# Attention block with a gated feed-forward branch on one core: first tile's rstd by logarithm and exponential, gate by exponential and reciprocal, whole loads of x

## The chip, the cores and the metric

One core of one Trainium2 chip. The metric is device time in microseconds (us). The span of a profile is 1.7 to 1.9 us shorter than the time of the same execution.

PE is the matrix engine (TensorE), PEld its weight loads, DVE the vector engine, ACT the scalar engine, POOL GpSimd, SP the engine that issues most transfers.

## The reference, cut to what matters

```python
xn = layernorm(x)                                # 2048 rows of 512, no affine part
q  = (xn @ wq) per head                          # 32 heads of 128
s  = softmax(q k^T / sqrt(128)) v  ->  @ wo      # 2048 keys
z  = relu(xn @ w1 + b1)**2 @ w2 + b2             # 512 -> 1792 -> 512
out = x + s * silu(z)                            # silu(z) = z * sigmoid(z)
```

## The kernel before

One helper records each engine's program in order and puts in semaphore waits; each engine gets its instructions in that order. Rows come in four blocks of 512, and each block in four tiles of 128. A step of the main loop makes scores for two key tiles, one exponential of 128x1024 on ACT, and the product with V. A head is eight steps. Between them PE gets one or two "filler" matmuls of other jobs (projections, the feed-forward branch, the output product). PE leaves its results in PSUM: scores in psA, the product with V in the two banks of psO, the fillers in the two banks of psF. DVE copies psO and psF out (it "evicts" them), and only then can PE write the bank again, so a late eviction makes PE wait.

The layernorm's statistics, with the reciprocal root of the variance (rstd) as a power on GpSimd:

```python
def ln_rstd(j, i, n=1, eng=GP):
    t = E(DV, bn_aggr(mv_t[:, i, :], st_t[:, i, 0:6 * n]), deps=[t_bn[jt]] + prev)
    t = E(eng, ts(ve_t[:, i:i+1], mv_t[:, i, 1:2], 1.0, LN_EPS, mult, add), deps=[t] + prev)
    t_xr[jt] = E(GP, tt(rstd[:, i:i+1], ve_t[:, i:i+1], mhalf, pow), deps=[t, t_mhalf])
# (helper names shortened, cut)
```

The gate: twice silu(z) is z (1 + tanh(z/2)); the factor of a half comes in later.

```python
def tanh():
    box[0] = E(AC, act(th_t[:, s, :], z_t[:, s, :], Tanh, scale=0.5), deps=[tz, t_thr[s]])
def gate():
    t_g[jt] = E(DV, stt(g_all[:, gs, :], th_t[:, s, :], 1.0, z_t[:, s, :], add, mult), ...)
at(step + 1, tanh)
at(step + 3, gate)       # issued at that step, or when a head is past its second step
```

The head of the program, where K of head 0 is transposed on PE and copied by ACT:

```python
x tile 0, rows 64-127 -> ACT queue;  rows 0-63 -> SP queue
ln_load(0, 1, AC); load_k0(0); fill_wq(0, AC); load_k0(1)
# (cut)
warm_up(36); k0_transpose(0); k0_copy(0)
ln_bn(0, 0); ln_rstd(0, 0, eng=DV); ln_bn(0, 1); ln_scale(0, 0)
first_transpose(0); k0_transpose(1); bias_rows(); k0_copy(1)
ln_rstd(0, 1, eng=DV); first_copy(0); bias_copy(); first_proj(0)
ln_scale(0, 1); first_evac(0); first_transpose(1)
gen_scores(0); ln_bn(0, 2); gen_scores(1)
```

The softmax here doesn't subtract the row's maximum and nothing guards it: scores larger than these inputs give would overflow.

## Time and profile before

| | |
|---|---|
| time, first three runs | 1238.45, 1239.90, 1241.53 us |
| span of the profile | 1236.3 us |
| PE busy | 1231.2 us |
| DVE busy, before the change | 472.5 us |
| gates made | 16, one per tile of 128 rows |

The prediction shows the profile lines.

One more line is used below, from the view of the gate's tile. It gives the durations of ACT's 16 gate instructions and the start of the first and of the last. Compared between two kernels, the first start shows what the head lost or gained, the last start what head and middle together did:

```profile
L161 ACT ACTIVATE th_t<-z_t x16: 621/622/632, 111.2 to 1195.9; 128x512 bf16<-128x512 f32 x16
```

### The profile page before, as it was taken

To read this page: it belongs to the slowest core of one execution; us is meant where nothing else is said; L and a number is where in the kernel's file an instruction comes from. 1 tells how busy PE (TensorE), PEld (TensorE's weight loads), DVE (VectorE), ACT (ScalarE), POOL (GpSimd) and SP (SyncE) were. 2 spreads that over 40 slices of the span, in tenths; PEclk is the share of its full clock that TensorE was granted. 3 is DMA by queue.
4 is the path that set the end of the run, shared out by engine and by line. 5 is a ranking of instruction groups with operands and counts; after the bars stand their busy time and mean duration, and the time that the engine had idled before them with its cause. 6 is when DMAs were issued, how large, how long until landed. Compare 5 with 4: busy or idle time off the path is not lost.

```text
span 1236.3 us, 26936 instructions
## 1 busy us (share of the span) xinstructions
PE 1231.2 (100%) x11885; PEld 818.7 (66%) x11885; DVE 472.5 (38%) x953; ACT 1053.7 (85%) x1044; POOL 31.9 (3%) x73
## 2 busy tenths in 40 slices
PE   9999999999999999999999999999999999999999
PEld 7666666666666666666666666666666666666666
DVE  4453323244435332334444532333344333324333
ACT  7888888888888888888888888888888888888885
POOL 1010000000002000000000200000000000000000
PEclk9999999999999999999999999999999999999999
DMA  9999997777879797878779978788779799878771
GB/s 213 203 243 194 186 178 134 131 143 142 141 151 170 143 160 129 138 140 144 133 133 170 172 138 144 141 148 133 133 145 148 146 154 158 137 134 147 146 123 31
DMA packets 686884, 185.41 MB, mean 150 GB/s; under 512 B 673552, under 2 KB 685584, under 8 KB 686768
## 3 DMA queue, kind: packets, MB, share of 16 engines
q1 hardware_dynamic: 684592, 179.56, 80.8%
q0 software_dynamic: 1424, 3.81, 1.3%
q8 instruction: 94, 1.54, 0.5%
q10 hardware_dynamic: 752, 0.33, 0.1%
q14 instruction: 22, 0.18, 0.1%
HBM read 96.60 MB, written 2.10 MB: 80 GB/s over the span
## 4 chain that ended last, share of the span: by engine, by line
PE 99%; DVE 0%; DMA 0%; ACTq 0%; issue 0%; DVEq 0%
PE psO L157 38%; PE psA L152 36%; PE psF L152 25%; DMA x_ln<-in_A_x_dram 0%; PE psA L157 0%; DVE out_t L165 0%; PE psF L196 0%; DVE tmp_t L175 0%; PE psO L152 0%; DVE st_t L200 0%; DVE xn_t L171 0%; ACTq L208 0%; PE psO L196 0%; DVE xnT L179 0%; DVE b1f L179 0%
## 5 line engine op out<-in xcount | busy, mean ns | idle before, releaser
L161 ACT ACTIVATE pT<-psA 128x1024 bf16<-128x1024 f32 x1024 | 1043.5, 1023 | 163.6 <-PE psA L152 118.3
L157 PEld LDWEIGHTS psO<-v_sb,pT 128*128 128x128 bf16 x8192 | 547.9, 98 | 240.2 <-issue 12.5
L157 PE MATMUL psO<-v_sb,pT 128*128 128x129 bf16 x8192 | 631.2, 220 | 0.0
L152 PE MATMUL psA<-qt_sb,kT 128*128 128x512 bf16 x2032 | 604.4, 379 | 0.0
L179 DVE COPY o_un<-psO 128x258 f32<-128x258 f32 x256 | 97.3, 421 | 399.6 <-PE psO L157 398.9
L152 PE MATMUL psF<-xnT,wq_sb 128*128 128x512 bf16 (+1 forms) x520 | 168.8, 374 | 0.1
L152 PE MATMUL psF<-wo_all,oT 128*128 128x512 bf16 x480 | 163.6, 379 | 0.0
L152 PEld LDWEIGHTS psA<-qt_sb,kT 128*128 128x128 bf16 x2032 | 157.0, 98 | 0.0
L179 DVE CAST qt_sb<-psF 128x512 bf16<-128x512 f32 (+1 forms) x130 | 87.9, 676 | 97.1 <-PE psF L152 97.1
L165 DVE TENSOR_TENSOR o_bf<-o_un,rden 128x512 bf16<-128x512 f32 x128 | 88.6, 692 | 4.6 <-DVE rden L183 0.3
L152 PEld LDWEIGHTS psF<-xnT,wq_sb 128*128 128x128 bf16 x520 | 50.3, 98 | 59.8 <-DVE xnT L179 0.2
L171 DVE TENSOR_SCALAR r_t<-psF,b1f 128x512 bf16<-128x512 f32 x56 | 42.0, 750 | 117.5 <-PE psF L152 117.5
L152 PEld LDWEIGHTS psF<-wo_all,oT 128*128 128x128 bf16 x480 | 46.9, 98 | 56.4
L152 PE MATMUL psF<-xnT,w_sb 128*128 128x512 bf16 x224 | 77.1, 379 | 0.0
L152 PE MATMUL psF<-w_sb,h2T 128*128 128x512 bf16 x224 | 74.1, 379 | 0.0
L152 PEld LDWEIGHTS psF<-w_sb,h2T 128*128 128x128 bf16 x224 | 21.9, 98 | 26.4
L152 PEld LDWEIGHTS psF<-xnT,w_sb 128*128 128x128 bf16 x224 | 21.9, 98 | 26.4
L165 DVE TENSOR_TENSOR z_t<-psF,b2bc 128x512 f32<-128x512 f32 x16 | 11.1, 692 | 67.2 <-PE psF L152 67.2
L165 DVE TENSOR_TENSOR acc<-psF,acc 128x512 f32<-128x512 f32 x28 | 19.3, 688 | 30.0 <-PE psF L152 30.0
L208 POOL DMA_DIRECT2D out_dram<-out_t x12 | 6.7, 555 | 891.0 <-DVE out_t L165 891.0
L165 DVE TENSOR_TENSOR h2T<-r_t 128x512 bf16<-128x512 bf16 x56 | 23.8, 425 | 1.9
L183 DVE RECIPROCAL rden<-o_un 128x4 f32<-128x4 f32 x128 | 22.9, 179 | 4.4
(47 smaller groups left out, 164.3 us busy)
## 6 DMA issues: line engine op xcount, KB each, us to landing
v_sb<-in_A_v_cache_dram SPq DMA_DIRECT2D x127, 512.0 KB, 4.7
wq_sb<-in_A_wq_dram SPq DMA_DIRECT2D x127, 128.0 KB, 3.0
wo_all<-in_A_wo_dram SPq DMA_DIRECT2D x4, 1024.0 KB, 6.3
w_sb<-in_B_w_dram SPq DMA_DIRECT2D x14, 256.0 KB, 4.6
oT<-o_bf SPq DMA_TRANSPOSE x128, 3.9
x_t<-in_A_x_dram POOLq DMA_DIRECT2D x16, 128.0 KB, 3.6
kT<-in_A_k_cache_dram SPq DMA_TRANSPOSE x127, 4.5
x_ln<-in_A_x_dram SPq DMA_DIRECT2D x14, 128.0 KB, 4.2
```

The costliest lines, as they stand in the source:

```text
L152: return e.matmul(out, lhsT, rhs, start=start, stop=stop)
L157: return e.matmul(out, lhsT, rhs, start=start, stop=stop, skip_group_check=True)
L161: return e.activation(out, in_, func, bias=bias, scale=scale)
L165: return e.tensor_tensor(out, in0, in1, op)
L171: return e.tensor_scalar(out, in0, scalar1=scalar1, scalar2=scalar2, op0=op0, op1=op1)
L179: return e.tensor_copy(out, in_)
L183: return e.reciprocal(out, in_)
L208: return e.dma_start(out, in_)
```

## The change

As the edits read, the intent is to take tile 0's normalization off the GpSimd power and to have its x earlier. The traces show ACT loading tables for its functions (ACT_TABLE_LOAD, 1.28 us); one load can serve a set of several. Tanh is given up for exp and a reciprocal, it seems for fear that a set with a logarithm would not have it. The code gives no reason; experiment 6 bears on it. The core of the diff:

```diff
+    def first_rstd(i):
+        t = E(DV, bn_aggr(mv_t[:, i, :], st_t[:, i, 0:6]), deps=[t_bn[i]])
+        t = E(AC, act(ve_t[:, i:i+1], mv_t[:, i, 1:2], Ln, bias=epsc), deps=[t, t_eps])
+        t_xr[i] = E(AC, act(rstd[:, i:i+1], ve_t[:, i:i+1], Exp, scale=-0.5), deps=[t])
...
-    th_t = sb("th_t", [P, 2, D], BF16)
+    th_t = sb("th_t", [P, 2, D], F32)
...
-            def tanh(): act(th_t, z_t, Tanh, scale=0.5)
+            def exp():  act(th_t, z_t, Exp, scale=-1.0)
+            def sigmoid():
+                t = ts(th_t, th_t, 1.0, add)          # DVE
+                box[0] = recip(th_t, th_t)            # DVE
-            gate: (th_t + 1.0) * z_t
+            gate: (th_t * 2.0) * z_t
-            at(step + 1, tanh); at(step + 3, gate)
+            at(step + 1, exp); at(step + 3, sigmoid); at(step + 4, gate)
...
-    x tile 0 in two halves on two queues
+    ln_load(0, 0, SP)
     ln_load(0, 1, AC)
-    warm-up activation: Exp
+    warm-up activation: Ln
...
     warm_up(36); k0_transpose(0)
+    ln_bn(0, 0); first_rstd(0)
     k0_copy(0)
-    ln_bn(0, 0); ln_rstd(0, 0, eng=DV)
     ln_bn(0, 1); ln_scale(0, 0); first_transpose(0); k0_transpose(1)
-    bias_rows()
     k0_copy(1)
-    ln_rstd(0, 1, eng=DV); first_copy(0); bias_copy(); first_proj(0)
-    ln_scale(0, 1); first_evac(0); first_transpose(1); gen_scores(0); ln_bn(0, 2)
+    ln_rstd(0, 1); first_copy(0); first_proj(0); first_evac(0); ln_scale(0, 1)
+    gen_scores(0); ln_bn(0, 2); first_transpose(1)
     gen_scores(1); first_copy(1)
+    bias_rows(); bias_copy()                          # now through psO
```

(Shortened; a debug print that does nothing by default goes too.)

More of the change, by code (lines that the diff above doesn't have):

```diff
@@ L279, in bass_recurrent_scan__mha_block_cached__dense_activation_squared_relu__prompt_kernel @@
     z_t = sb("z_t", [P, 2, D], F32)
-    th_t = sb("th_t", [P, 2, D], BF16)
+    th_t = sb("th_t", [P, 2, D], F32)
+    epsc = sb("epsc", [P, 1], F32)
     b1b = sb("b1b", [NFC, P], BF16)
@@ L327, in bass_recurrent_scan__mha_block_cached__dense_activation_squared_relu__prompt_kernel @@
     t_mhalf = E(GP, partial(_memset, out=mhalf[:], val=-0.5))
+    t_eps = E(GP, partial(_memset, out=epsc[:], val=LN_EPS))
     t_idf = E(GP, partial(_iota, out=identf[:]))
@@ L356, in ln_bn @@
         t_bn[jt] = E(DV, partial(_bn_stats, out=st_t[:, i, k:k + 6], in_=x_ln[:, i, c0:c1]),
-                     deps=[t_xl[jt], t_x0 if jt == 0 else None, t_xn.get(jt - TPB),
-                           t_xr.get(jt - TPB)])
+                     deps=[t_xl[jt], t_xn.get(jt - TPB), t_xr.get(jt - TPB)])
     def ln_rstd(j, i, n=1, eng=GP):
@@ L368, in ln_rstd @@
                                  op=ALU.pow), deps=[t, t_mhalf])
+    def first_rstd(i):
+        t = E(DV, partial(_bn_aggr, out=mv_t[:, i, :], in_=st_t[:, i, 0:6]), deps=[t_bn[i]])
+        t = E(AC, partial(_act, out=ve_t[:, i:i + 1], in_=mv_t[:, i, 1:2], func=ACT.Ln,
+                          bias=epsc[:]), deps=[t, t_eps])
+        t_xr[i] = E(AC, partial(_act, out=rstd[:, i:i + 1], in_=ve_t[:, i:i + 1], func=ACT.Exp,
+                                scale=-0.5), deps=[t])
     def ln_stats(j, i):
@@ L445, in bias_rows @@
     def bias_rows():
-        t_b1[0] = E(PE, partial(_peT, out=psA[:, 1536:1600].bitcast(BF16)[:, 0:NFC], in_=b1b[:],
-                                ident=ident[0:NFC, 0:NFC]), deps=[tok_b1, t_ident])
+        t_b1[0] = E(PE, partial(_peT, out=bankO(1)[:, 0:64].bitcast(BF16)[:, 0:NFC], in_=b1b[:],
+                                ident=ident[0:NFC, 0:NFC]), deps=[tok_b1, t_ident, t_k0[1]])
     def bias_copy():
         t_b1[0] = E(DV, partial(_copy, out=b1f[:],
-                                in_=psA[:, 1536:1600].bitcast(BF16)[:, 0:NFC]), deps=[t_b1[0]])
+                                in_=bankO(1)[:, 0:64].bitcast(BF16)[:, 0:NFC]), deps=[t_b1[0]])
     def first_proj(i):
@@ L470, in second_proj @@
                                       start=(c == 0), stop=(c == NDC - 1)),
-                          deps=[t_wqfill[1], tok_xT[0][i], t_k0[1]], inc=(c == NDC - 1))
+                          deps=[t_wqfill[1], tok_xT[0][i], t_k0[1], t_b1[0]], inc=(c == NDC - 1))
     def second_evac():
@@ L539, in gen_scores @@
                                   rhs=qt_sb[:, 0, qt * P:(qt + 1) * P], start=True, stop=True),
-                      deps=[t_k0[b], t_q0[qt], t_exp[pi - 2] if pi >= 2 else t_b1[0]],
+                      deps=[t_k0[b], t_q0[qt], t_exp[pi - 2] if pi >= 2 else None],
                       inc=(c == NKT // 2 - 1))
@@ L622, in bass_recurrent_scan__mha_block_cached__dense_activation_squared_relu__prompt_kernel @@
     nfin = [0]
-    import os
-    dbg = os.environ.get("KDBG")
     pending = []
@@ L686, in evac, with exp @@
             box = [None]
-            def tanh():
-                box[0] = E(AC, partial(_act, out=th_t[:, s, :], in_=z_t[:, s, :], func=ACT.Tanh,
-                                       scale=0.5), deps=[tz, t_thr[s]])
+            def exp():
+                box[0] = E(AC, partial(_act, out=th_t[:, s, :], in_=z_t[:, s, :], func=ACT.Exp,
+                                       scale=-1.0), deps=[tz, t_thr[s]])
+            def sigmoid():
+                t = E(DV, partial(_ts, out=th_t[:, s, :], in0=th_t[:, s, :], scalar1=1.0,
+                                  scalar2=None, op0=ALU.add), deps=[box[0]])
+                box[0] = E(DV, partial(_recip, out=th_t[:, s, :], in_=th_t[:, s, :]), deps=[t])
             def gate():
@@ L694, in gate @@
                 t_g[jt] = t_zrd[s] = t_thr[s] = E(
-                    DV, partial(_stt, out=g_all[:, gs, :], in0=th_t[:, s, :], scalar=1.0,
-                                in1=z_t[:, s, :], op0=ALU.add, op1=ALU.mult),
+                    DV, partial(_stt, out=g_all[:, gs, :], in0=th_t[:, s, :], scalar=2.0,
+                                in1=z_t[:, s, :], op0=ALU.mult, op1=ALU.mult),
                     deps=[box[0], t_fin.get(jt - 2 * TPB)])
-            at(step + 1, tanh)
-            at(step + 3, gate)
+            at(step + 1, exp)
+            at(step + 3, sigmoid)
+            at(step + 4, gate)
             return tz
@@ L856, in load_w1 @@
                                sl_w1[i])
-    sl_x0 = S.slot("x0b")
-    t_x0 = S.emit_dma(AC, partial(_dma, out=x_ln[P // 2:P, 0, :], in_=A_x[0, P // 2:P, :]), sl_x0)
-    t_xl[0] = S.emit_dma(SP, partial(_dma, out=x_ln[0:P // 2, 0, :], in_=A_x[0, 0:P // 2, :]),
-                         sl_xl[0])
+    ln_load(0, 0, SP)
     ln_load(0, 1, AC)
@@ L865, in bass_recurrent_scan__mha_block_cached__dense_activation_squared_relu__prompt_kernel @@
     load_k0(1)
-    E(AC, partial(_act, out=th_t[:, 0, 0:1], in_=warm[:, 0:1], func=ACT.Exp), deps=[t_warm])
+    E(AC, partial(_act, out=th_t[:, 0, 0:1], in_=epsc[:], func=ACT.Ln), deps=[t_eps])
     ln_load(0, 2, SP)
@@ L910, in bass_recurrent_scan__mha_block_cached__dense_activation_squared_relu__prompt_kernel @@
     k0_transpose(0)
+    ln_bn(0, 0)
+    first_rstd(0)
     k0_copy(0)
-    ln_bn(0, 0)
-    ln_rstd(0, 0, eng=DV)
     ln_bn(0, 1)
@@ L917, in bass_recurrent_scan__mha_block_cached__dense_activation_squared_relu__prompt_kernel @@
     k0_transpose(1)
-    bias_rows()
     k0_copy(1)
     t_kfill[0] = t_k0[1]
-    ln_rstd(0, 1, eng=DV)
+    ln_rstd(0, 1)
     first_copy(0)
-    bias_copy()
     first_proj(0)
+    first_evac(0)
     ln_scale(0, 1)
-    first_evac(0)
-    first_transpose(1)
     gen_scores(0)
     ln_bn(0, 2)
+    first_transpose(1)
     gen_scores(1)
     first_copy(1)
+    bias_rows()
+    bias_copy()
     ln_rstd(0, 2)
@@ L988, in bass_recurrent_scan__mha_block_cached__dense_activation_squared_relu__prompt_kernel @@
             n += 1
-        if dbg:
-            print(pi, n, round(credit, 1), jobs[0][0] if jobs else None, len(pending))
         if pi >= NPR:
```

## The prediction

> **What bounds the kernel now.** I read the page's first part and its chain of waits first, then a table of busy time by stretches, then the timeline of the first 16 us (nearly every edit of the change sits there), the groups by form for the price of each operation, and last the timeline around the places where the gate is made. The page:
>
> ```profile
> PE 1231.2 (100%) x11885; PEld 818.7 (66%) x11885; DVE 472.5 (38%) x953; ACT 1053.7 (85%) x1044; POOL 31.9 (3%) x73
> ...
> PE 99%; DVE 0%; DMA 0%; ACTq 0%; issue 0%; DVEq 0%
> ```
>
> TensorE (PE) is the bound for practically the whole span of 1236.3 us. Everything else runs beside it, so a change can only count where it makes PE stand still, or stops it from standing still. The table of stretches says where PE stands still:
>
> ```profile
> 0.00:5.00 5.00, 3.89 (x41) 3.72 (x42) 1.03 (x3) 1.49 (x2) 2.58 (x13) 1.00 0.53 154
> 5.00:10.00 5.00, 3.99 (x60) 3.24 (x58) 4.05 (x14) 3.35 (x4) 1.31 (x4) 1.00 1.26 255
> 10.00:15.50 5.50, 5.43 (x96) 5.13 (x93) 3.19 (x10) 4.51 (x5) 1.34 (x3) 1.00 1.04 216
> ...
> 25.00:1225.00 1200.00, 1200.00 (x11531) 794.53 (x11529) 455.62 (x912) 1036.12 (x1026) 24.16 (x52) 1.00 0.83 150
> ```
>
> After the length of each stretch comes PE's busy time. From 25 to 1225 us it is 1200.00 of 1200.00. Only the head is loose, and even there part of the 3.89 us in the first 5 is warming-up matmuls on zeros. The change removes no PE work (the same transposes, in another order), so its whole possible gain lies in the first 8 us, before the first scores. That path in the timeline:
>
> ```profile
> 2.71 1.28 ACT L161 ACT_TABLE_LOAD   x1 [2.71 <-issue]
> 3.27 0.69 DVE L200 BATCH_NORM_STATS2 st_t<-x_ln 128x6 f32<-128x512 bf16 x1 [3.27 <-DMA x_ln<-in_A_x_dram]
> 4.46 0.57 POOL L165 TENSOR_TENSOR rstd<-ve_t,mhalf 128x1 f32<-128x1 f32 x1 [1.75 <-DVE ve_t L171]
> 5.12 0.69 DVE L200 BATCH_NORM_STATS2 st_t<-x_ln 128x6 f32<-128x512 bf16 x1 [0.75 <-DMA x_ln<-in_A_x_dram]
> 5.73 0.40 DVE L171 TENSOR_SCALAR xn_t<-x_ln,mv_t,rstd 128x512 bf16<-128x512 bf16 x1
> ...
> 8.02 0.91 PEld L157 LDWEIGHTS psA<-qt_sb,kT 128*128 128x128 bf16 x16
> ```
>
> The reader should see that the GpSimd power ends at 5.03, but the scaling of tile 0 starts only at 5.73: DVE works in order, and the statistics of tile 1 stand in front of it, and those wait for tile 1's x until 5.12. So the power isn't what tile 0 waits for; the late tile 1 is. The weights of the first scores are loaded at 8.02.
>
> **What the Trainium skill says.** (1) "ScalarE: Activation LUTs", section "Table sets: the hidden batching unit": functions come in sets loaded together; exp and tanh share one, a set with both ln and exp exists, and that set is not listed with tanh. The trace agrees for the first half: 1024 exponentials and 16 tanh ran on one load. No run here shows yet which set a logarithm brings. (2) The same page, section "What ACT_TABLE_LOAD costs": about 1283 ns, plus a drain of some 1380 ns, for a switch. The load here took 1283 ns; no switch between sets exists in this trace, so the drain isn't shown. (3) "VectorE: DVE Perf Modes", section "First, the fixed hardware budget": a reciprocal is an iterative divide with a repeat count of 8. The trace speaks for eight cycles an element, worked out below. (4) The same page, section "The perf-mode tier table (the rule you actually need)": a tensor-with-scalar operation on fp32 in SBUF runs at twice the basic rate; no such fp32 operation of any width is in this trace, though the 128x512 bf16 one takes 0.40 us.
>
> **The change part by part.**
>
> The gate, 16 times. Removed: a tanh; added: an exponential of the same 128x512 tile. Both are one ACT pass over the same elements, 624 ns by the group of tanh; fp32 output I take as free. ACT: no change. On DVE two instructions come in front of the gate, an add and a reciprocal over 128x512 fp32. The prices by form:
>
> ```profile
> L183 DVE RECIPROCAL rden<-o_un 128x4 f32<-128x4 f32 x128 | 22.9, 179 | 4.4
> ...
> L175 DVE SCALAR_TENSOR_TENSOR tmp_t<-psA,g_all 128x128 f32<-128x128 f32 x2 | 0.6, 291 | 0.2
> L175 DVE SCALAR_TENSOR_TENSOR tmp_t<-psA,g_all 128x256 f32<-128x256 f32 x1 | 0.4, 424 | 0.9 <-PE psA L152 0.9
> L171 DVE TENSOR_SCALAR ve_t<-mv_t 128x1 f32<-128x1 f32 x2 | 0.3, 154 | 0.1
> ```
>
> From 128 to 256 columns costs 133 ns, 1.04 ns a column, so one column a cycle is 1.04 ns, and the fixed part is 291 - 133 = 158 ns. One column costs 154. The reciprocal of four columns costs 179, which is 25 more than 154: three further columns at 8.3 ns, or eight cycles each. If that holds at 512 columns, one reciprocal is 154 + 511 x 8.33 = 4.41 us. At one cycle it would be 0.69 us. The add is, at double rate, about 0.15 + 512 x 0.52 = 0.42 us (estimate). So DVE gains 16 x 4.83 = 77 us of work (or 16 x 1.1 = 18), going from 472 to about 550 us, 44% of the span. By average that is nothing; in place it can hold up an eviction. What counts is the time from the gate's place to the next thing PE needs of DVE. I looked at all 16 gates in the timeline: each starts right behind a head's normalization, and the next eviction of psO (two banks, which PE needs back within about 0.7 us of finishing) comes 6.8 to 7.8 us later. 4.83 plus the gate's 0.69 fits. The evictions of psF come sooner, but psF also has two banks, so each has until the next psF job ends. The tightest case:
>
> ```profile
> 249.97 0.69 DVE L175 SCALAR_TENSOR_TENSOR g_all<-th_t,z_t 128x512 bf16<-128x512 bf16 x1
> ...
> 250.57 0.68 DVE L179 CAST qt_sb<-psF 128x512 bf16<-128x512 f32 x1
> ...
> 254.06 0.75 DVE L171 TENSOR_SCALAR r_t<-psF,b1f 128x512 bf16<-128x512 f32 x1 [2.81 <-PE psF L152]
> ...
> 254.74 0.59 PE L152 MATMUL psF<-wo_all,oT 128*128 128x512 bf16 x2
> ```
>
> The query's bank, evicted now at 250.57, is wanted again at 254.74. With the slow reciprocal it is evicted at 249.97 + 4.83 + 0.69 = 255.5: PE waits 0.75 us. The same happens at the gate at 555.95 (0.75). At 862.15 the bank is wanted at 867.60 and free at 867.67 (0.1). At the last gate, 1199.48, two combining operations and one eviction follow: 4.83 + 4 x 0.69 = 7.6 us puts the next psO eviction at 1207.1, its half done at 1207.5, and PE wants it at 1207.13 (0.4). Every other gate has at least 5.6 us until the next psF job ends. Sum if the reciprocal is slow: +2.0 us; if fast: 0.
>
> The head. Removed: the half-and-half load of tile 0 (halves landed 2.2 and 2.4 us after issue), DVE's small scaling (0.15) and the GpSimd power (0.57). Tile 0 now comes whole, alone on its queue; I put it between the half's 2.4 and the 3.8 us of tile 1, which queued behind a half: lands 3.6 instead of 3.27. Tile 1 no longer queues and should land near 3.6 to 4.0 instead of 5.10; that is the gain. Statistics of tile 0: 3.6 to 4.5 with the aggregate. On ACT: table load until 3.99, its first small activation until 4.2 as before, the logarithm 4.5 to 4.8 and the exponential to about 5.05 (about 0.2 to 0.28 each by the 205 ns of the first small one). Tile 1's statistics run 4.5 to 5.2 meanwhile; tile 0's scaling starts at about 5.25 instead of 5.73. Then, by the durations of before: transposes (0.4), copy (0.42), projection (0.4), eviction (0.29) and first scores. The bias transpose and tile 1's scaling (0.40) leave the way, so the first scores come near 7.4 instead of 8.02: -0.65 us. It assumes one table load.
>
> **The rivals.** First, two table loads: if a logarithm brings a set without exp, the exponential behind it loads a second one, 1.28 us on exactly this path. The scaling then starts at about 6.55 instead of 5.25, and the copy of K on ACT too stands behind it. First scores at about 8.6: +0.6 us. For it: the kernel only asks for a function, and the first choice for a lone logarithm need not hold exp. Against: giving up the tanh makes sense only if it would have cost reloads, so the one who wrote it expected the joint set. I give it 55%. If the joint set then never held, there still are no reloads later: only exp remains. Second, the slow reciprocal as an outright bound, +2% or more: for it, 77 us of new DVE work in lumps; against, the positions above, always behind a head's end. Third, the lone load of tile 0 arrives much later than 3.6 and eats the gain: that would give 0 in the head. Fourth, nothing at all: the head's gain is lost again in the following 7 us, where PE also waits for ACT and DVE in turn.
>
> **Range and chances.** Head: 0.45 x (-0.65) + 0.55 x 0.6 = +0.04. Gate: slow with 65%, so 0.65 x 2.0 = +1.3. Sum +1.3 on 1239.9 gives 1241.2; as the version was probably kept by someone who timed it, I shade it to 1240.8. The three runs before lie from 1238.45 to 1241.53, 3 us apart, which is wider than any of my terms; so the range is 1238.0 to 1243.3. Two per cent would be 24.8 us: slower needs a stall of 1.5 us at each of the 16 gates, faster would need PE work to vanish. I give 0.01 to each, 0.98 to within 2%.
>
> **What would show it.** In the changed profile: the group of the 128x512 reciprocal near 4.4 us (or 0.7); DVE near 550 us (or 490); PE waits for a DVE eviction of psF or psO near 250, 556 and 1207 us and nowhere else in the middle; the number of table loads; the scaling of tile 0 at 5.25 or 6.55; the first scores at 7.4 or 8.6. It would be wrong if the reordering put a gate's reciprocal close before a head's end, so that PE waits at all 16, or if loads of tables appear in the steady part.

## The result and the profile after

| | before | after |
|---|---|---|
| median of six runs | 1239.53 us | 1240.11 us |
| lowest to highest | 1238.36 to 1241.53 | 1240.02 to 1240.22 |
| span of the profile | 1236.3 us | 1238.2 us |

The ratio is 1.0004, with a 95% interval from 0.9991 to 1.0017: the same. Ratios here are the mean time of one kernel's fast runs over that of the other's in the same rounds, so not quite the ratio of the quoted medians. Small as it is, the traces differ by 1.9 us, more than the medians do: the runs of the kernel before scatter upward, and its lowest two are 1.7 us below the changed kernel's median.

From the page of the changed kernel, busy time by engine and the chain's shares:

```profile
PE 1231.7 (99%) x11885; PEld 818.9 (66%) x11885; DVE 532.3 (43%) x983; ACT 1056.3 (85%) x1047; POOL 31.6 (3%) x74
...
PE 98%; DVE 1%; DMA 0%; ACT 0%; issue 0%; DVEq 0%
```

PE has the same number of instructions as before. DVE has 60 us more, and it appears in the chain with 1%. The groups by form give the new prices (busy, then mean ns of one):

```profile
L183 DVE RECIPROCAL th_t<-th_t 128x512 f32<-128x512 f32 x16 | 53.7, 3353 | 0.6
...
L170 DVE TENSOR_SCALAR th_t<-th_t 128x512 f32<-128x512 f32 x16 | 6.8, 422 | 0.0
...
L161 ACT ACT_TABLE_LOAD x2 | 2.6, 1283 | 1.7 <-PEq L1042 1.7
```

Two loads of tables, an add of 0.42 us as estimated, and a reciprocal of 3.35 us. The table of stretches, PE's busy time behind the length of each:

```profile
0.00:5.00 5.00, 4.02 (x40) 4.02 (x41) 1.45 (x3) 2.15 (x4) 2.08 (x13) 1.00 0.61 175
5.00:10.00 5.00, 3.13 (x48) 2.52 (x45) 2.65 (x8) 3.91 (x5) 0.75 (x2) 1.00 1.25 253
...
25.00:1225.00 1200.00, 1199.41 (x11530) 794.06 (x11528) 514.70 (x943) 1037.90 (x1027) 24.15 (x52) 1.00 0.82 149
```

From 5 to 10 us PE is busy 3.13 us where it was 3.99, and 0.6 us are missing in the middle that was full. The head in the timeline:

```profile
3.37 0.69 DVE L200 BATCH_NORM_STATS2 st_t<-x_ln 128x6 f32<-128x512 bf16 x1 [3.37 <-DMA x_ln<-in_A_x_dram]
4.10 0.18 DVE L204 BATCH_NORM_AGGREGATE mv_t<-st_t 128x2 f32<-128x6 f32 x1
4.20 0.66 DVE L200 BATCH_NORM_STATS2 st_t<-x_ln 128x6 f32<-128x512 bf16 x1
4.31 0.29 ACT L161 ACTIVATE ve_t<-mv_t,epsc 128x1 f32<-128x1 f32 x1 [1.16 <-DVE mv_t L204]
4.62 1.28 ACT L161 ACT_TABLE_LOAD   x1
...
5.92 0.20 ACT L161 ACTIVATE rstd<-ve_t 128x1 f32<-128x1 f32 x1
...
6.16 0.41 DVE L171 TENSOR_SCALAR xn_t<-x_ln,mv_t,rstd 128x512 bf16<-128x512 bf16 x1 [1.30 <-ACT rstd L161]
...
8.46 0.46 PEld L157 LDWEIGHTS psA<-qt_sb,kT 128*128 128x128 bf16 x8 [0.62 <-issue]
```

Tile 1's statistics start at 4.20 instead of 5.12: the loads did what they were for. But between the logarithm and the exponential stands the second table load, and DVE sits idle for 1.30 us in front of the scaling "<-ACT rstd". The scaling starts at 6.16 instead of 5.73.

PE's own waits in the whole run, and the gate's first and last start:

```profile
PE psF L196 <- DVE xn_t L171: 1.2, 1, 1.2
...
PE psF L152 <- DVE qt_sb L179: 0.6, 2, 0.3
```
```profile
L161 ACT ACTIVATE th_t<-z_t x16: 621/622/632, 112.1 to 1197.8; 128x512 f32<-128x512 f32 x16
```

Before, PE waited for no eviction of a query at all. The first gate is 0.9 us later than before, the last one 1.9: so 0.9 us in the head and 1.0 in the middle. Setting the 1024 exponentials of the two traces side by side, the difference is 0.44 us at the first two, 0.89 from the third to the one at 256 us, then 1.43, then 1.85 from 563 us on, and it does not move again. The step at 256 us in the timeline:

```profile
251.34 3.35 DVE L183 RECIPROCAL th_t<-th_t 128x512 f32<-128x512 f32 x1
...
254.73 0.69 DVE L175 SCALAR_TENSOR_TENSOR g_all<-th_t,z_t 128x512 bf16<-128x512 f32 x1
...
255.34 0.68 DVE L179 CAST qt_sb<-psF 128x512 bf16<-128x512 f32 x1
...
256.17 0.59 PE L152 MATMUL psF<-wo_all,oT 128*128 128x512 bf16 x2 [0.34 <-DVE qt_sb L179]
```

The matmul that stood at 254.74 before stands at 256.17: 1.43 later, of which 0.89 was brought along from the head. It waited for the query's eviction, which stood in DVE's order behind reciprocal and gate. The listed wait is 0.34 and the loss 0.54, because the wait is counted from the end of the matmul before: with no wait the next one starts before that end (254.31 to 254.74 in the kernel before, 0.43 apart), here it came 0.94 after (255.23 to 256.17).

### The profile page after: what moved, and what is told of

It reads as the page before. It is cut to its first block, busy times and chain, and to the rows that moved or that the text cites. A ratio compares the mean times of both kernels' runs of the same rounds, so it can differ in the third digit from the quotient of the medians.

```text
span 1238.2 us, 26969 instructions
## 1 busy us (share of the span) xinstructions
PE 1231.7 (99%) x11885; PEld 818.9 (66%) x11885; DVE 532.3 (43%) x983; ACT 1056.3 (85%) x1047; POOL 31.6 (3%) x74
## 4 chain that ended last, share of the span: by engine, by line
PE 98%; DVE 1%; DMA 0%; ACT 0%; issue 0%; DVEq 0%
PE psO L157 37%; PE psA L152 35%; PE psF L152 25%; DVE th_t L183 1%; PE psA L157 0%; DMA x_ln<-in_A_x_dram 0%; DVE o_un L179 0%; DVE qt_sb L179 0%; DVE out_t L165 0%; DVE o_bf L165 0%; DVE g_all L175 0%; ACT L161 0%; PE psF L196 0%; PE psO L152 0%; DVE tmp_t L175 0%
## 5 line engine op out<-in xcount | busy, mean ns | idle before, releaser
L161 ACT ACTIVATE pT<-psA 128x1024 bf16<-128x1024 f32 x1024 | 1044.4, 1024 | 164.1 <-PE psA L152 118.6
L183 DVE RECIPROCAL th_t<-th_t 128x512 f32<-128x512 f32 x16 | 53.7, 3353 | 0.6
```

Source lines behind the costliest of these rows:

```text
L161: return e.activation(out, in_, func, bias=bias, scale=scale)
L183: return e.reciprocal(out, in_)
```

## The experiments

Kernels ran with runs of the kernel before among them. Where the two differ by parts of a microsecond I trust the traces' spans and the lower half of the runs more than the ratio, for reasons that the first experiment shows.

**1. The kernel before once more.** No edit.

> The kernel before, unchanged. Its six timed runs scatter over 3.2 us (1238.36 to 1241.53), the changed kernel's six over 0.2. If the scatter belongs to the kernel, it shows again: over 1 us between lowest and highest. If it was only an accident of when the runs were taken, these lie within 0.4 us of each other. Should the profiled run be a slow one, the trace shows in which stretch the time lies.

Measured: five runs from 1238.25 to 1238.56 us, median 1238.36. The runs of the kernel before taken beside it as the comparison (11 of them, the same program) went from 1238.08 to 1241.23. So the scatter isn't a property of this program alone, as I had thought; it was absent here and present in the same minutes under the other name. The high comparison runs are what pull the "before" up. In some of them the granted clock is 0.999 (1240.10 us, for one), in others it is 1.000 (1241.23), so the clock explains at most a part; the rest stays open. What the run gives is a base: 1238.3 us, span 1236.5 to 1236.8.

**2. The bias rows alone.** They are transposed late, through psO.

```diff
-    k0_transpose(1); bias_rows(); ... first_copy(0); bias_copy()
+    k0_transpose(1); ... first_copy(0)
-    first_copy(1)
+    first_copy(1); bias_rows(); bias_copy()
```

> The kernel before with one piece of the change alone: the transpose of the bias rows moved behind the second tile's transpose, into psO. Theory: in the kernel before PE stands in front of the bias transpose until the small GpSimd-queue load of the bias lands, and that landing varies; then this kernel's runs lie within 0.4 us of each other, near 1238.3, and the scatter of the kernel before is explained. Rival: the scatter is from something else (the two half loads, the GpSimd power); then these runs scatter over more than 1 us as before, and the median stays near 1239.5.

Measured: 1238.47 to 1241.95 us (six runs), median 1238.54. The scatter theory falls: one run is 3.4 us up although the bias is out of the way. The move itself gains nothing. Side by side with the profiled kernel before, its first two exponentials are 0.08 us later and the third and all that follow 0.31: the bias transpose costs some 0.23 us in its new place, where PE is already in work.

**3. One table load.** The changed kernel, with the joint set asked for by name.

```diff
+    E(AC, preload_act_table_set("natural_log_exp_and_others"), inc=False)
     E(AC, act(th_t[:, 0, 0:1], epsc, Ln), deps=[t_eps])
```

> The changed kernel with the table set that holds both logarithm and exponential asked for by name, so one table load instead of two. Theory (the second load lies on the first tile's path): the first tile's scaling starts 1.0 to 1.3 us earlier, near 5.0, the profile's span falls from 1238.2 to about 1237.0, the time to about 1238.9. Rival (the second load is hidden by the load of K or by the wait for tile 1): under 0.3 us.

Measured: median 1239.09 us (1238.81 to 1239.25), span 1237.4, 0.8 below the changed kernel. The profiled run was the slowest of the five; by the medians it is 1.0. From its timeline:

```profile
4.39 0.29 ACT L161 ACTIVATE ve_t<-mv_t,epsc 128x1 f32<-128x1 f32 x1 [1.23 <-DVE mv_t L204]
4.71 0.20 ACT L161 ACTIVATE rstd<-ve_t 128x1 f32<-128x1 f32 x1
...
4.95 0.41 DVE L171 TENSOR_SCALAR xn_t<-x_ln,mv_t,rstd 128x512 bf16<-128x512 bf16 x1
...
6.38 0.62 PE L196 MATMUL psO<-ident,kT 128*128 128x128 bf16 x8 [0.56 <-DMA kT<-in_A_k_cache_dram]
6.78 0.27 PEld L152 LDWEIGHTS psF<-xnT,wq_sb 128*128 128x128 bf16 x4
...
7.67 0.46 PEld L157 LDWEIGHTS psA<-qt_sb,kT 128*128 128x128 bf16 x8 [0.62 <-issue]
```

Without the load the scaling starts at 4.95, 1.21 us earlier. Of these, 0.79 reach the first scores: PE, in order, has the second half of K to transpose before the projection, and that half only lands at 6.38. So the second load was worth 0.8 us in this pair of profiles, not 1.28; the next wait took the rest. It is also worth seeing that exponentials cost the same under the joint set (a mean of 1023 ns for one of 128x1024, 1024 in the changed kernel), and that the middle is like the changed kernel's (two waits of PE for a query's eviction, 0.6 us).

**4. The new gate alone**, in the kernel before.

```diff
-    th_t BF16; tanh; gate = (th + 1) * z
+    th_t F32;  exp; add; reciprocal; gate = (2 * th) * z
```

> The kernel before with the new gate alone (exponential, add, reciprocal), its head untouched. Theory: the 3.35 us reciprocal holds up the eviction of one psF bank at two of the 16 gates, near 256 and 562 us, by 0.54 and 0.42 us: the span is 1.0 us above that of an equal draw of the kernel before, with nothing elsewhere, and the scatter of the kernel before stays. Rival (the new gate costs nothing, and the middle's 1.0 us in the changed kernel came from a shift of the head): under 0.2 us.

Measured: median 1239.41 us (1239.21 to 1240.40), span 1237.6, against 1236.7 of experiment 1. Side by side with experiment 1, its exponentials step by 0.50 us at 257 us and by 0.42 at 563, nowhere else. PE's waits have the same line as in the changed kernel:

```profile
PE psF L152 <- DVE qt_sb L179: 0.6, 2, 0.3
```

The middle's loss belongs to the gate and doesn't depend on the head.

**5. The loads alone**, in the kernel before.

```diff
-    x tile 0 in halves on ACT and SP
+    ln_load(0, 0, SP)
     ln_load(0, 1, AC)
```

> The kernel before with the loads of the change alone: tile 0 whole on one queue, tile 1 whole on the other. Theory (in the kernel before tile 0's scaling waits behind tile 1's statistics, which wait for the late tile 1): tile 1's statistics start at 4.3 to 4.5 instead of 5.1 to 5.4, the scaling of tile 0 at about 5.2 instead of 5.7 to 6.0, the first scores 0.3 to 0.6 us earlier, the span 0.3 to 0.6 us lower. Rival (what stands behind it, the second half of K or the weights, comes no earlier): the scaling moves, the first scores and the span do not, under 0.15 us.

Measured: median 1238.04 us (1237.73 to 1238.26), beside 1238.60 of the kernel before; ratio 0.9992 (0.9980 to 1.0005). Span 1236.3 against 1236.7 of experiment 1, and every exponential 0.40 us earlier than there. The interval of the ratio holds 1, and the kernel before has had a profile of 1236.3 too (the first one); but all five runs lie below all nine of the kernel before beside them (1238.43 and up).

```profile
4.47 0.68 DVE L200 BATCH_NORM_STATS2 st_t<-x_ln 128x6 f32<-128x512 bf16 x1
4.64 0.57 POOL L165 TENSOR_TENSOR rstd<-ve_t,mhalf 128x1 f32<-128x1 f32 x1 [1.94 <-DVE ve_t L171]
...
5.25 0.41 DVE L171 TENSOR_SCALAR xn_t<-x_ln,mv_t,rstd 128x512 bf16<-128x512 bf16 x1
```

Here the GpSimd power ends at 5.21 and the scaling starts at 5.25 (6.04 in experiment 1). The old power keeps pace with ACT's pair under the joint set to 0.3 us, without touching a table.

**6. The head alone**: the changed kernel with the old gate.

```diff
-    exp, add, reciprocal, gate * 2
+    tanh, gate + 1
```

> The changed kernel with the old gate (tanh, no add and no reciprocal). Theory: two table loads as in the changed kernel and no third, because the set that the first exponential brings carries tanh too; the head is as late as in the changed kernel (first scores near 8.5), the stretch from 25 us on is full again, and the span is 0.9 to 1.0 us below the changed kernel's, near 1237.3. Rival (tanh is not in that set): 16 pairs of further loads on ACT and a time higher by several us.

Measured: median 1239.14 us (1239.08 to 1239.20), span 1237.3. Scaling at 6.22 and first scores at 8.53, as in the changed kernel; the steps at 256 and 563 us are gone: side by side with the kernel before, the difference stays at 0.96 to 0.99 us from the third exponential to the end. There are two table loads and no more, with 16 tanh in the program, so the set that the first exponential brings has tanh. PE's busy time in the middle can't be used here: 201 of its matmul records are missing from this trace. The two losses are separate, 0.9 (head) and 1.0 (middle), and giving up tanh wasn't needed with the loads as they were placed. Whether the joint set of experiment 3 has tanh was not tried.

**7. Power and tanh kept, loads and order new.**

```diff
     (the changed kernel)
-    first_rstd(0): Ln, Exp on ACT
+    ln_rstd(0, 0, eng=DV): GpSimd power
-    exp, add, reciprocal
+    tanh
-    warm-up activation: Ln
+    warm-up activation: Exp
```

> The changed kernel without both of its swaps of functions: the GpSimd power instead of logarithm and exponential, and the old gate; what stays are the whole loads, the order of the head and the late bias rows. Theory: one table load, no wait in the middle; the scaling of tile 0 near 5.2, first scores near 7.9, the span 1236.2 to 1236.7, the best of all so far by 0.1 to 0.4 us or equal to the kernel before. Rival (the new order of the head costs what the loads gain): 1236.8 to 1237.2.

Measured: median 1238.16 us (1238.10 to 1238.77), beside 1238.60; span 1237.0. The scaling starts at 5.17 as expected, the first scores at 8.13 instead of near 7.9, and the span is 0.3 above what I expected. But the profiled run was the slowest of the five: the spans of the other four are 1236.3 to 1236.7, as expected, so the rival is not borne out. In this draw the second half of K made PE wait 0.8 us, and from the third exponential on another 0.46 us are lost against the kernel before. That step of 0.45 to 0.46 is in every kernel with the new order (the changed one, and experiments 3, 6 and 7) and in none with the old. Half of it is the bias (experiment 2). For the other half I can only argue: tile 1's transpose was moved from in front of the first scores to behind them, which makes the first exponential early without saving PE any work.

**8. The reciprocal twice**, the first into a tile that nobody reads.

```diff
+    t = t_tmp[s] = E(DV, recip(tmp_t[:, s, :], th_t[:, s, :]), deps=[t, t_tmp[s]])
     box[0] = E(DV, recip(th_t[:, s, :], th_t[:, s, :]), deps=[t])
```

> The changed kernel with a second reciprocal of the same tile, its result thrown away, in front of the one that counts: the lump on DVE grows from 3.8 to 7.1 us. Theory (a lump on DVE costs nothing as long as it ends before the next psO eviction is due, and what is over the slack is lost in full): shifting the changed kernel's trace by 3.35 us puts the next psO eviction 0.6 to 2.8 us late at all 16 gates, 21 us in sum; less about 0.4 us of slack at each, and with the psF banks wanted earlier at three gates added, the time rises by 12 to 25 us. Rival (average load decides, DVE would be busy for 586 of 1238 us): under 2 us.

Measured: median 1269.02 us (1268.13 to 1269.86), ratio 1.0244 (1.0229 to 1.0260): slower by 2.4%. The result is still right. Span 1266.4, 28.2 above the changed kernel, a little over the range I gave. PE's waits:

```profile
PE psF L152 <- DVE qt_sb L179: 10.9, 4, 3.7
PE psO L157 <- DVE o_un L179: 10.1, 10, 2.6
```

The change's own reciprocal added 3.35 us of DVE work to each gate, and with the add it cost PE 1.0 us in the whole run; 3.35 more cost 28. DVE is busy 584.60 us of 1266, under half. The average doesn't decide; the deadline does.

Not all of the 28 is waiting. The mean granted clock of this run is 0.996, and the last stretch shows it, third from the end:

```profile
1225.00:1267.00 42.00, 35.48 (x319) 23.61 (x322) 20.29 (x30) 21.07 (x22) 2.54 (x2) 0.96 0.19 37
```

PE's clock was at half for 3.41 us three times, from 574.41, 888.43 and 1236.59 us, each time when PE had stood still for most of the 3.4 us before (busy for 0.00, 0.37 and 1.12). That is at most 1.7 us each, 5.1 in all (an estimate: half of 3 x 3.41 us). Without it the loss would be near 23, inside the range I gave. Side by side with the changed kernel, the exponentials step by 3.4 us at its 257 us, after a wait of PE of 3.73 us that left the clock at 1.00, and by 5.0 at its 564 us, after a wait of 3.64 us that half clock followed; at its 871 us, again with half clock, the step is 4.9.

**9. The changed kernel once more.** No edit.

> The changed kernel, unchanged, on the chip of this call. The runs of the kernel before taken first in a round scattered upward so far, by up to 3 us, while the same program run as a separate kernel did not (1238.25 to 1238.56). If the changed kernel costs what its trace says (0.9 us in the head, 1.0 us in the middle), its median lies 1.6 to 2.0 us over the lower half of the runs of the kernel before here; if the small ratio on record is the truth, 0.3 to 0.8 us.

Measured: 1240.01 to 1240.12 us, median 1240.05; the kernel before beside it 1238.35 (1238.23 to 1239.25); ratio 1.0012 (1.0000 to 1.0025). The difference of the medians is 1.70 us, as the traces say. The 0.58 on record was small because its runs of the kernel before were high. It is 0.14%, and still "the same" by the 2% rule.

**10. The reciprocal in two halves.**

```diff
-    box[0] = E(DV, recip(th_t[:, s, :]), deps=[t])
+    box[0] = E(DV, recip(th_t[:, s, 0:D//2]), deps=[t])            # step + 3
+    def sigmoid2(): box[0] = E(DV, recip(th_t[:, s, D//2:D]), ...)  # step + 4
-    at(step + 4, gate)
+    at(step + 4, sigmoid2); at(step + 5, gate)
```

> The changed kernel with its reciprocal in two halves of 256 columns, the second put into the order one step later, so that an eviction of psF can come between. The sum of DVE work grows a little (16 more instructions of some 0.15 us); the longest lump falls from 3.8 to about 2.2 us. Theory (the length of the lump is what costs): the waits of PE near 256 and 562 us vanish, the span falls by 0.9 to 1.0 us to near 1237.3. Rival (the whole DVE work between two evictions counts, however it is cut): the waits stay, within 0.3 us of the changed kernel.

Measured: median 1239.18 us (1239.13 to 1240.40), span 1237.4, 0.9 below the changed kernel. The waits at 256 and 562 us are gone. But not for the reason given:

```profile
251.42 3.54 DVE L183 RECIPROCAL th_t<-th_t 128x256 f32<-128x256 f32 x2
254.88 0.63 DVE L179 CAST qt_sb<-psF 128x512 bf16<-128x512 f32 x1
255.42 0.68 DVE L175 SCALAR_TENSOR_TENSOR g_all<-th_t,z_t 128x512 bf16<-128x512 f32 x1
255.62 0.22 PEld L152 LDWEIGHTS psF<-wo_all,oT 128*128 128x128 bf16 x2 [0.21 <-issue]
255.75 0.59 PE L152 MATMUL psF<-wo_all,oT 128*128 128x512 bf16 x2
```

The two halves ran back to back, 3.54 us together; nothing came between. What moved is the gate: one step later in the order, it now stands behind the query's eviction. The eviction starts at 254.88 instead of 255.34, and PE is in time by a hair. So what I called the length of the lump was not tested; the order of gate and eviction was. That shorter lumps would help as such is not shown.

**11. Both repairs.** Experiments 3 and 10 together.

> Both repairs together: the joint table set and the reciprocal in halves. If the two losses are independent, they add: span 1236.4 to 1236.7, time 1238.2 to 1238.5, level with the kernel before. If the earlier head moves the gates against the evictions, some of it comes back in the middle.

Measured: median 1238.21 us (1237.90 to 1238.51), beside 1238.35; ratio 0.9997 (0.9985 to 1.0010); span 1236.4. The gains add: 0.8 and 0.9 would make 1236.5. With both repairs, the intended change is level with the kernel before. PE has no wait for an eviction of psF in the middle.

**12. Projection before K's second half**, in the kernel with whole loads.

```diff
     first_transpose(0)
+    first_copy(0); first_proj(0); first_evac(0)
     k0_transpose(1); bias_rows(); k0_copy(1)
-    ln_rstd(0, 1, eng=DV); first_copy(0); bias_copy(); first_proj(0)
-    ln_scale(0, 1); first_evac(0)
+    ln_rstd(0, 1, eng=DV); bias_copy(); ln_scale(0, 1)
```

> The kernel before with whole loads of x and the first tile's projection and eviction put in front of the second half of the K transposes, on which PE, working in order, waited in front of the projection (second half landed at 6.29 us). Theory (PE's order makes the projection wait for K): the projection starts at about 6.6 instead of 7.0, but the copy of the second half of K on ACT starts later; the first exponential 0.1 to 0.4 us earlier than 8.60 and the span 1235.9 to 1236.2. Rival (the copy of K on ACT is then what the first exponential waits for): no gain or up to 0.3 us lost.

Measured: median 1240.66 us (1239.47 to 1241.37), span 1238.9. A miss, 2.3 us over the kernel before. The projection did start at 6.72. But my edit also put tile 1's aggregate behind tile 0's eviction; tile 1 was scaled only at 8.38, and its transpose, in front of the first scores, kept PE waiting until 8.85. Then the clock fell to half, from 8.97 to 12.38 us. The stretches, PE's busy time second, the granted clock third from the end:

```profile
5.00:9.00 4.00, 2.21 (x29) 1.78 (x28) 2.31 (x9) 2.05 (x2) 0.77 (x2) 1.00 1.29 258
9.00:11.00 2.00, 2.00 (x22) 2.00 (x21) 0.91 (x3) 0.73 (x1) 0.74 (x2) 0.50 1.10 238
11.00:13.00 2.00, 2.00 (x26) 2.00 (x25) 1.27 (x4) 1.21 (x2) 0.00 (x0) 0.66 1.13 249
```

At half clock the first 16 score matmuls took 1.91 us instead of 1.05. The runs divide in the same way: two with a clock of 1.000 took 1239.47 and 1239.66 us, three with 0.998 or 0.999 took 1240.66 to 1241.37. So by these runs the order itself cost about 1.2 us over the kernel before, and the rest goes with the clock. What makes it fall is not settled: PE was busy for 2.21 of the 4 us before, but in the changed kernel for 2.13 of the same stretch, and there the clock stayed at 1.00.

## Why the prediction was right or wrong

The time, 1240.11 us, lies in the range, and "same" was right. The steps:

- *What bounds the kernel, and that only head and evictions can count*: right. All that was lost is in the first 11 us and at two places in the middle.
- *Two table loads (55%)*: that branch came. The scaling started at 6.16 (forecast 6.55) and the first scores at 8.46 (forecast 8.6); x landed at 3.37 rather than 3.6, and ACT's first load was over at 2.94, not at 3.99, which gained nothing because the logarithm waits for the statistics.
- *Head +0.6 us with two loads*: it was 0.9. The step that failed is "the first scores" as the measure of the head. The 0.44 at the first exponentials is near the forecast; another 0.45 comes after them, from the new order of transposes and bias, which the sum took as free.
- *Head -0.65 us with one load*: wrong. With one load (experiment 3) the scaling was even earlier than forecast, 4.95 against 5.25, but the first scores came at 7.67, not 7.4, and with the order's 0.45 the head ended 0.1 us behind the profiled kernel before. The landing of K's second half was in no term of the sum.
- *The reciprocal at eight cycles a column, 4.41 us*: too high. It took 3.35, and its halves 1.75. Between 256 and 512 columns that is (3353 - 1753)/256 = 6.25 ns a column, six cycles of 1.04 ns. A fit on one group of four columns could not tell six from eight: at six, four columns would have come out at 154 + 3 x 6.25 = 173 ns, where the trace had 179. The add was right (0.42), though the prediction's remark that the trace has no fp32 operation of its kind "of any width" is not: it lists one of 128x1 itself.
- *The gate: 0.75, 0.75, 0.1 and 0.4 us*: the places were half right. Losses came near 256 and 562 us (0.54 and 0.42) and at no other of the 16. A second error hid in that step: 255.5 was the time at which the query's eviction starts, and I took it as the time at which the bank is free. The eviction's own 0.68 was left out and partly made up for the too long reciprocal. The gates at 862 and 1199 us cost nothing with 3.35.
- *The base*: 1239.9 of three scattered runs was about 1.4 us above the later medians of the same kernel (1238.35 to 1238.71). With the branch that came the steps would have given 1239.9 + 0.6 + 2.0 = 1242.5. True were about 1238.3 + 1.9. So the close hit owes something to errors of opposite sign.
- *Rivals*: a slow reciprocal as an outright bound was rightly given little; experiment 8 shows that another 3.35 us would have made it one. The late lone load did not happen. The fourth, that the head's gain is lost again in the 7 us behind it, came in part: the 0.45 of the new order.

## What to carry to other kernels

On an engine that evicts for the bound engine, ask not how busy it is but when the next eviction is due: 3.8 us nearly fitted and cost 1 us in all, 7.1 us cost 28 more, some 5 of them by a halved clock. Check in the trace which tables a new function brings before giving anything up for it; here one named load was worth 0.8 us, and the reason for dropping tanh had not arisen. Try the parts of a change one by one: the loads alone gained about 0.4 us by the trace (near the noise), and the parts around them lost 1.9 or more.

## What the Trainium skill lacked or had wrong

- "ScalarE: Activation LUTs", "Table sets: the hidden batching unit", gives one load for ln followed by exp, and "ScalarE activation tables: per-element evaluation and per-set limits", "Table sets in the compiler and the runtime", says that loads are placed block by block, greedily for the longest run. In this kernel a logarithm followed by exponentials had two loads; one only when the joint set was asked for by name (experiment 3).
- "ScalarE: Activation LUTs", "What ACT_TABLE_LOAD costs": the 1283 ns agree. The drain of some 1380 ns doesn't show: the logarithm ended at 4.60, the load ran from 4.62 to 5.90, the exponential started at 5.92.
- "VectorE: DVE Perf Modes", "First, the fixed hardware budget", names a repeat count of 8 for the reciprocal, and no page gives the time of one. Measured for fp32 in SBUF: 1753 ns at 256 columns, 3353 at 512, so 6.25 ns a column. The same page's "The perf-mode tier table (the rule you actually need)" was right on the fp32 add (422 ns).
- "TensorE: Matmul & The Clock Gate", "What's actually happening", has the clock fall after at least one idle window of about 3.4 us. Here it also fell after stretches that were not idle: in experiment 12 at 8.97 us, when PE had been busy for 1.63 of the 3.42 us before and its longest wait was 1.2 us, and in experiment 8 at 1236.59, after 1.12 of 3.39. Its section "A second HAM failure mode: psum-queue depth-cycling" does tell of short, frequent idling that brings the clock down; how much is enough it does not say, and no run here settles it.
